# Three small moves of order in a fused attention and MLP kernel: one W2 sum, one z transpose, and the tail loads

## The chip, the cores and the metric

The kernel runs on one core of a Trainium2 chip. The metric is the device time of one execution in microseconds (us), the median over the runs of a kernel. A core has TensorE (PE in the profile; its weight loads are listed apart as PEld), VectorE (DVE), ScalarE (ACT), GpSimd (POOL) and SyncE (SP). Each works through its own instructions in the order in which they were issued; semaphores hold an instruction back until what it needs is done. Here SP issues nearly all of the DMA transfers.

## The reference

Eight batches of 576 positions, eight heads of 64. The first half is causal attention in a window of 64 keys; the second is a layer norm, two matrix products with a ReLU between them, and a residual sum.

```python
# q, k, v: [8, 8, 576, 64] float32
scores = q @ k.T / sqrt(64);  keep 0 <= (query - key) < 64, else -1e9
x = softmax(scores) @ v                    # -> [8, 576, 512], heads side by side
xn = (x - mean(x)) / sqrt(var(x) + 1e-6) * g_ln
out = x + relu(xn @ w_ch1) @ w_ch2         # w_ch1 [512, 2048], w_ch2 [2048, 512]
```

## The kernel before

**Groups.** The rows are worked on in nine groups. Groups 0 to 7 are the first 512 rows of each batch, as four row blocks (`kb`) of 128. Group 8, the "last group", gathers the remaining 64 rows of all eight batches, again as four row blocks, each of two batches; these are the "tails" 0 to 3.

**What one group needs.** For a batch: `load_qk` and `load_v` bring the float32 inputs, `cast_qk` and `cast_v` turn them into float16 on POOL, and `t_main` transposes q and k, on TensorE with an eviction by ACT or DVE, or for q from batch 3 on with a DMA that transposes on its way through the crossbar (L265). `s_pe` makes the scores (L349), `s_exp` the exponentials on ACT, `s_mask` the window on DVE, `b_pe` the product with v (L396); `part_vB` makes a shifted copy of v by DMA (L201, L203). `b_mult` and `b_stats` on DVE divide by the sums and take mean and variance; `z_step` on POOL writes the normalised rows z (L448 to L454). `zt_step` transposes z into `zT[g]`, the operand of the MLP: for groups 0 and 1, and for block 3 of groups 2, 3 and 5, with four TensorE transposes into one PSUM tile and a copy out of it (L478, L481 on ACT or L483 on DVE), for all other blocks with a crossbar DMA (L474).

**The MLP of a group.** It is a list of units (`mlp_units`): first the products with W1 (`l1`, L501; or in halves, `l1_half`, L642), then the products with W2. From group 1 on the W2 product is done with seven block products in place of eight (`stage` n, p, L575), which needs sums of blocks of the hidden rows (`s_sums`, L549) and of W2 (`w2_sums`, L836, into the tiles wT2, wT3 and wT4; the third of them, number 4, is made of W2 and of sum 2). The tiles wT2 to wT4 are also the landing place of three raw parts of W2, so that a sum can only be written after POOL has cast that part. The sums of the first half of the columns are made in group 0, those of the second half in group 1.

**The order.** A loop over the groups writes the order out by hand: `at(i, f, ...)` puts a piece of work for the next batch behind unit i of the present group. In group 2 the units 0 to 15 are the halves of W1, and 16 to 29 are the fourteen stages. So `at(22, ...)` of group 2 stands behind stage (6, 0), and the block transposes and tails that follow are for group 3, which is batch 3. Group 2 also carries the loads, casts and transposes of batch 4, and, as the last group's tail 0 is worked on in group 3, the work `load_tail`, `cast_tail` and `t_tail` for tail 0.

**PSUM for transposes.** `t_tile` gives out the tiles t0 and t1 in turn. From unit 20 on (17 in group 0) `tbank["shared"]` is set and it always gives t0, since t1 is then an accumulator of the W2 stages.

**DMA order on SP.** All the transfers named above stand in one queue on SP. Their completion is told by eight semaphores in turn, so each transfer is issued only after the one eight places ahead of it has landed. In group 2 the queue reads, in order: the loads of batch 4, the crossbar transfer of z block 0 of group 3, the six loads of tail 0 (L104 to L106), two crossbar transfers of q of batch 4 (L265), those of z blocks 1 and 2 (L474), the copies of v (L201, L203), four stores (L536), and the loads of batch 5.

Of the kernel before, what the change touches and what calls it, by code (L numbers as in the profile page):

```python
# [18 lines left out]
def kernel(  # L19
# [10 lines left out]
    nc = tc.nc  # L30
    B, H, S, D = q.shape
    DM = H * D
    HID = 4 * DM
    SM = 512
# [6 lines left out]
    XZ = 2  # L41
# [30 lines left out]
    def t_tile(shape, name):  # L72
        i = 0 if tbank["shared"] else tbank["n"] % 2
        tbank["n"] = i + 1
        return ps_t.tile(shape, FP16, tag=f"t{i}", name=name)
# [21 lines left out]
    def load_tail(i):  # L97
        tq = p_in.tile([128, H, D], FP32, tag="tq32", name=f"tq32_{i}", bufs=1)
        tk = p_in.tile([128, 2, H, D], FP32, tag="tk32", name=f"tk32_{i}", bufs=1)
        tv = p_in.tile([128, 2, H, D], FP32, tag="tv32", name=f"tv32_{i}", bufs=1)  # L100
        tail32[i] = (tq, tk, tv)
        for r in range(2):
            b = 2 * i + r
            nc.sync.dma_start(out=tq[64 * r:64 * r + 64], in_=q[b, :, SM:S, :].rearrange("h s d -> s h d"))  # L104
            nc.sync.dma_start(out=tk[:, r], in_=k[b, :, S - 128:S, :].rearrange("h s d -> s h d"))
            nc.sync.dma_start(out=tv[:, r], in_=v[b, :, S - 128:S, :].rearrange("h s d -> s h d"))  # L106

    def cast_tail(i):
        tq, tk, tv = tail32.pop(i)
# [358 lines left out]
    def zt_step(g, kb, eng="act"):  # L468
        z = zsd.pop((g, kb))
        if g not in zT:  # L470
            sfx = "r" if g == NGRP - 1 else ""
            zT[g] = p_grp.tile([128, NKC, 512], FP16, tag="zT" + sfx, name=f"zT_{g}", bufs=1 if sfx else 2)
        if XZ <= g and not (kb == 3 and g in (2, 3, 5)):
            nc.sync.dma_start_transpose(out=zT[g][:, :, 128 * kb:128 * kb + 128], in_=z)  # L474
            return
        ztp = t_tile([128, NKC, 128], f"ztp_{g}_{kb}")
        for kc in range(NKC):
            nc.tensor.transpose(out=ztp[:, kc, :], in_=z[:, 128 * kc:128 * (kc + 1)], identity=ident16)  # L478
        dst = zT[g][:, :, 128 * kb:128 * kb + 128]
        if eng == "act":  # L480
            nc.scalar.copy(out=dst, in_=ztp)  # L481
        else:
            nc.vector.tensor_copy(out=dst, in_=ztp)  # L483
# [362 lines left out]
    for i in range(8):  # L846
# [8 lines left out]
        out=mask[0:64], in_=mask[0:64], compare_op=ALU.is_gt, fill=0.0,  # L855
# [3 lines left out]
        out=mask[64:128], in_=mask[64:128], compare_op=ALU.is_ge, fill=0.0,  # L859
# [48 lines left out]
    b_step(0, 1)  # L908
    t_main(0, 1, 1, 0)
    zt_step(0, 0, "dve")  # L910
    keep_clock(2)
    s_mm(0, 2, True)
    zt_step(0, 1, "dve")
    keep_clock(1)
    b_step(0, 2)
# [31 lines left out]
    for g in range(NGRP):  # L947
# [7 lines left out]
        def at(i, f, *a):  # L955
            slots[min(i, len(slots) - 1)].append((f, a))
# [9 lines left out]
        b = g + 1  # L966
        if g == 0:
            at(0, w1_cast, 3, (1,), True)
            at(0, queue_up)
            at(1, zt_step, 0, 2, "dve")  # L970
            at(2, zt_step, 0, 3, "dve")
            at(11, t_main, 1, 0, 0, 1)
            at(12, t_main, 1, 1, 0, 1)
            at(16, s_pe, 1, 0)
            at(16, s_pe, 1, 1, False, "xps")
            at(16, s_exp, 1, 0, 0, 1)
            at(16, s_mask, 1, 0)
            at(17, s_exp, 1, 1, 0, 1)
            at(17, s_mask, 1, 1)
            for c in range(2):  # L980
                at(20, vB_cur, 1, c, 0)
                at(20, vB_prev, 1, c, 0)
            for i in (3, 2, 4):
                at(20, w2_sums, i, 0, 4)
            at(22, b_pe, 1, 0)
            at(22, b_rows, 1, 0)
            at(22, z_step, 1, 0)
            at(22, cast_act, 1, 0, 1)
            at(22, z_act, 1, 0)
            at(22, cast_qk, 1, 1, (1,))  # L990
            at(22, load_qk, 2, 1)
            at(22, load_v, 2, 0, 4)
            at(23, b_pe, 1, 1, "sc")
            at(23, b_rows, 1, 1)
            at(23, z_step, 1, 1)
            at(23, cast_v, 1, 2, 3)
            at(23, shift_v, 64, 2)
            at(23, shift_v, 0, 2)
            at(23, cast_v, 1, 3, 4)
            at(23, shift_v, 64, 3)  # L1000
            at(25, t_main, 1, 0, 1, 0)
            at(25, z_dve, 1, 1)
            at(26, lambda: tbank.update(n=0))
            at(26, t_main, 1, 1, 1, 0)
            at(27, zt_step, 1, 0, "dve")
            at(27, s_pe, 1, 2)
            at(27, s_pe, 1, 3, False, "xps")
            at(27, s_exp, 1, 2, 0, 1)
            at(27, s_exp, 1, 3, 0, 1)
            at(28, zt_step, 1, 1, "dve")  # L1010
            at(29, s_mask, 1, 2)
            at(29, s_mask, 1, 3)
        if g == 1:
# [38 lines left out]
            for j in range(4):  # L1052
                i = (13, 16, 22, 22)[j]
# [5 lines left out]
                i = (13, 17, 25, 27)[j]  # L1059
# [26 lines left out]
        if g == 2:  # L1086
            at(0, load_qk, 4, 1)
            at(0, s_exp, 3, 1, 1)
            at(1, z_act, 2, 3)
            at(1, s_mask, 3, 1)  # L1090
            at(2, b_pe, 3, 0)
            at(2, s_pe, 3, 2)
            at(2, s_pe, 3, 3, False, "t")
            at(5, zt_step, 2, 3, "act")
            for i, x in zip((2, 3, 4, 6), ((3, 0), (3, 1), (2, 0), (2, 1))):
                at(i, s_exp, 3, *x)
            at(3, load_v, 4, 0, 4)
            at(4, s_mask, 3, 3)
            at(4, b_rows, 3, 0)
            at(4, z_step, 3, 0)  # L1100
            at(7, s_mask, 3, 2)
            at(7, alloc_qkT, 4)
            at(7, after_mask, 3, 2)
            at(7, cast_qk, 4, 0)
            at(7, cast_qk, 4, 1)
            for j in range(1, 4):
                at(9, b_pe, 3, j, ("xps", "t", "sc")[j - 1])
                at((9, 10, 11)[j - 1], b_rows, 3, j)
                at((9, 10, 11)[j - 1], z_step, 3, j)
            for j, i in enumerate((8, 14, 18, 25)):  # L1110
                at(i, zt_step, 3, j)
        elif g > 1 and b < B:
            tail = TAILS.get(g)
            at(2, b_pe, b, 0)
            at(2, b_rows, b, 0)
            at(2, z_step, b, 0)
            at(2, s_pe, b, 2)
            at(2, s_exp, b, 2, 0, 1)
            at(3, s_mask, b, 2)
            if tail:  # L1120
                r, i = NGRP - 1, tail[0]
                at(2, s_pe, r, i, False, "t")
                at(4, s_exp, r, i, 0)
                at(5, s_exp, r, i, 1)
                at(5, s_mask, r, i)
                at(7, b_pe, b, 1)
                at(7, b_pe, r, i, "t")
                at(7, s_mm, b, 3)
                at(7, b_rows, b, 1)
                at(7, z_step, b, 1)  # L1130
                at(8, s_mask, b, 3)
                at(8, b_rows, r, i)
                at(9, z_step, r, i)
                at(12, b_pe, b, 2)
                at(12, b_pe, b, 3, "sc")
                at(16, zt_step, r, i)
            else:
                at(2, s_pe, b, 3, False, "t")
                at(4, s_exp, b, 3, 0)
                at(5, s_exp, b, 3, 1)  # L1140
                at(5, s_mask, b, 3)
                at(7, b_pe, b, 1)
                at(7, b_pe, b, 2, "t")
                at(7, b_pe, b, 3, "sc")
                at(7, b_rows, b, 1)
                at(7, z_step, b, 1)
            if g + 2 < B:
                at(5, alloc_qkT, g + 2)
                at(5, after_mask, *((NGRP - 1, tail[0]) if tail else (b, 3)))
                at(5, cast_qk, g + 2, 0)  # L1150
                at(5, cast_qk, g + 2, 1, (0,))
                at(11, cast_qk, g + 2, 1, (1,))
            for j, i in ((2, 12), (3, 19)):
                at(i, b_rows, b, j)
                at(i, z_step, b, j)
            for j in range(4):
                at((2, 14, 18, {3: 25, 5: 25}.get(b, 23))[j], zt_step, b, j)
# [7 lines left out]
        n = g + 2  # L1165
# [23 lines left out]
                at((15, 15, 20, 22)[i - 1], s_sums, 6, 8, i)  # L1189
        for n, i in enumerate(TAILS.get(g + 1, ())):  # L1190
            if n == 0:
                at(9 if g == 2 else 4, load_tail, i)
                at(24 if i < 2 else 18, cast_tail, i)
                at(27 if i < 2 else 22, t_tail, i, 0)
                at(29 if i < 2 else 22, t_tail, i, 1)
            else:
                at(25, load_tail, i)
# [48 lines left out]
```

## Time and profile before

| | us |
|---|---|
| median of 3 runs (lowest to highest) | 300.29 (299.87 to 301.8) |
| the profiled execution, its own time | 300.63 |
| its span, first to last instruction | 298.9 |
| PE busy in the span | 290.4 (97%) |
| DVE, POOL, ACT busy | 217.3, 163.1, 154.0 |
| mean granted TensorE clock | 0.998 |

The profile shows one execution. Busy time of an engine is the time in which at least one of its instructions ran; PE's matmuls are pipelined, so the time of a row of matmuls is read from the start of the first to the start of what follows. A timeline line gives the start, the length, the engine, the line of the code, the operation and its tiles, how many instructions are merged, and in brackets the engine's idle time before it with what ended that. For SP a line is the issue of a transfer, not its landing.

### The profile page before, as it was taken

The numbers are of one execution on the slowest core, as the hardware profiler recorded it, in microseconds if no ns is written. First come the engines' busy times: TensorE is split into PE (matmuls) and PEld (weight loads), VectorE is DVE, ScalarE is ACT, GpSimd is POOL, SyncE is SP. The second block draws the span as 40 slices with busy tenths as digits, with TensorE's granted clock in tenths as the row PEclk, the third lists the DMA queues.
The fourth block names the chain that finished last, engine by engine and source line by source line (L and its number), as shares of the span: only waits on it lengthen the run. The fifth ranks groups of instructions, "written<-read, shape, count | busy, mean of one in ns | idle before, by whom it ended". The sixth has DMA issues, their size and how long they took to land.

```text
span 298.9 us, 7820 instructions
## 1 busy us (share of the span) xinstructions
PE 290.4 (97%) x3183; PEld 206.4 (69%) x3183; DVE 217.3 (73%) x414; ACT 154.0 (52%) x260; POOL 163.1 (55%) x243
## 2 busy tenths in 40 slices
PE   7889999999999999999999999999999999999993
PEld 3557545888888888457854786469646854788883
DVE  2771388799993894489767865699568785779982
ACT  4576647677449525773276428841674056306500
POOL 4688877753850987189508860897048407024300
PEclk9999999999999999999999999999999999999999
DMA  7999999969979999999299998991729497003014
GB/s 190 260 380 339 385 283 280 261 213 301 181 170 290 246 174 161 271 272 180 45 285 279 190 174 278 285 162 39 220 52 179 71 177 195 20 18 143 1 37 106
DMA packets 113767, 58.24 MB, mean 195 GB/s; under 512 B 83137, under 2 KB 104705, under 8 KB 113730
## 3 DMA queue, kind: packets, MB, share of 16 engines
q1 hardware_dynamic: 113296, 57.34, 81.0%
q8 instruction: 25, 0.41, 0.6%
q10 hardware_dynamic: 434, 0.40, 0.4%
q14 instruction: 12, 0.10, 0.1%
HBM read 38.80 MB, written 9.44 MB: 161 GB/s over the span
## 4 chain that ended last, share of the span: by engine, by line
PE 66%; DMA 14%; DVE 8%; POOL 5%; SPq 3%; issue 2%; ACT 0%; POOLq 0%; DVEq 0%
PE hps L501 24%; PE pA L575 11%; PE pB L575 7%; PE pC L575 7%; DMA qk<-in_k_dram 6%; DMA w2s<-in_moe_w_ch_dram 3%; PE xps L396 3%; PE lA L698 2%; PE hph L642 2%; PE sc L349 2%; DMA out_dram<-xn 2%; POOL qk L154 2%; PE tp L276 2%; DMA tk<-in_k_dram 2%; DMA zT<-z 1%
## 5 line engine op out<-in xcount | busy, mean ns | idle before, releaser
L501 PE MATMUL hps<-zT,w1g 128*128 128x512 f16 x352 | 80.2, 379 | 0.4 <-DMA zT<-z 0.4
L505 ACT ACTIVATE hrT<-hps 128x512 f16<-128x512 f32 x88 | 52.8, 600 | 37.3 <-PE hps L501 34.3
L501 PEld LDWEIGHTS <-w1g 128*128 128x128 f16 x352 | 33.1, 98 | 38.6 <-issue 1.7
L575 PEld LDWEIGHTS <-sS 128*128 128x128 f16 x512 | 49.3, 98 | 5.7
L359 ACT ACTIVATE pt<-sc 128x512 f16<-128x512 f32 x72 | 39.8, 602 | 22.6 <-PE sc L349 22.1
L448 POOL TENSOR_SCALAR rsz<-mvg 128x1 f32<-128x1 f32 x32 | 10.5, 328 | 66.0 <-DVE mvg L429 63.4
L575 PEld LDWEIGHTS <-hrT 128*128 128x128 f16 x384 | 36.7, 98 | 7.0 <-ACT hrT L505 0.8
L369 DVE TENSOR_TENSOR pt<-pt,mask 128x1024 f16<-128x1024 f16 x32 | 24.4, 769 | 19.6 <-ACT pt L359 19.6
L642 PE MATMUL hph<-zT,w1g 128*128 128x256 f16 x320 | 38.0, 273 | 0.0
L154 POOL CAST qk<-qk 128x1024 f16<-128x1024 f32 x29 | 32.6, 1145 | 9.1 <-PE sc L349 6.0
L642 PEld LDWEIGHTS <-w1g 128*128 128x128 f16 x320 | 30.4, 98 | 4.7 <-POOL w1g L230 0.3
L575 PE MATMUL pC<-w2s,sS 128*128 128x256 f16 x256 | 31.1, 273 | 0.0
L575 PE MATMUL pA<-wT,sS 128*128 128x256 f16 x256 | 30.9, 273 | 0.0
L647 ACT ACTIVATE hrT<-hph 128x512 f16<-128x512 f32 x40 | 24.1, 606 | 11.0 <-PE hph L642 10.7
L257 ACT COPY qkT<-tp 128x1024 f16<-128x1024 f16 (+1 forms) x18 | 17.3, 963 | 23.2 <-PE tp L276 22.3
L549 DVE TENSOR_TENSOR sS<-hrT 128x1024 f16<-128x1024 f16 (+2 forms) x41 | 26.2, 638 | 2.1 <-ACT hrT L505 2.0
L420 DVE TENSOR_TENSOR xn<-xps,rcp 128x256 f32<-128x256 f32 (+1 forms) x50 | 25.8, 539 | 1.6 <-DMA out_dram<-xn 0.9
L426 DVE BATCH_NORM_STATS2 stats<-xn 128x6 f32<-128x512 f32 x36 | 25.0, 694 | 1.2
L454 POOL TENSOR_SCALAR z<-xn,rsz 128x512 f16<-128x512 f32 x24 | 22.4, 932 | 2.5
L449 POOL TENSOR_TENSOR rsz<-rsz,mhalf 128x1 f32<-128x1 f32 x32 | 20.6, 642 | 2.7
L182 POOL CAST vA<-v 128x1024 f16<-128x1024 f32 (+1 forms) x18 | 16.7, 945 | 4.2 <-DMA v<-in_v_dram 4.0
L416 DVE RECIPROCAL rcp<-xps 128x4 f32<-128x4 f32 (+1 forms) x50 | 7.9, 179 | 14.4 <-PE xps L396 14.4
(120 smaller groups left out, 421.9 us busy)
## 6 DMA issues: line engine op xcount, KB each, us to landing
qk<-in_q_dram SPq DMA_DIRECT2D x16, 512.0 KB, 6.0
qk<-in_k_dram SPq DMA_DIRECT2D x16, 512.0 KB, 6.9
out_dram<-xn SPq DMA_DIRECT2D x32, 256.0 KB, 3.6
v<-in_v_dram SPq DMA_DIRECT2D x28, 256.0 KB, 7.4
w2s<-in_moe_w_ch_dram SPq DMA_DIRECT2D x9, 512.0 KB, 8.5
w1s<-in_moe_w_ch_dram SPq DMA_DIRECT2D x4, 512.0 KB, 7.3
tk<-in_k_dram SPq DMA_DIRECT2D x8, 256.0 KB, 4.8
tv<-in_v_dram SPq DMA_DIRECT2D x8, 256.0 KB, 5.2
```

The lines of the kernel that those rows point to most:

```text
L154: nc.gpsimd.tensor_copy(out=dst[:, :].rearrange("p (a j) e d -> p a e j d", j=j), in_=t[:, :].rearrange("p (a e j d) -> p a e j d", e=2, j ...
L359: nc.scalar.activation(out=o, in_=i, func=AF.Exp, bias=0.0, scale=scale)
L369: nc.vector.tensor_tensor(out=ptv, in0=ptv, in1=mb, op=ALU.mult)
L420: nc.vector.tensor_tensor(out=xn[:, n * i:n * i + n], in0=xps[:, :, 0:D], in1=rcp_b, op=ALU.mult)
L426: nc.vector.bn_stats(out=stats, in_=xv)
L454: nc.gpsimd.tensor_scalar(out=z, in0=xv, scalar1=rs, scalar2=nm, op0=ALU.mult, op1=ALU.add)
L501: nc.tensor.matmul(out=hps, lhsT=w1g[:, kc, 128 * hc:128 * (hc + 1)], rhs=zT[g][:, kc, :], start=(kc == 0), stop=(kc == NKC - 1),)
L505: nc.scalar.activation(out=hrT[:, hc, :], in_=hps, func=AF.Relu, bias=0.0, scale=1.0)
L549: nc.vector.tensor_tensor(out=o, in0=x, in1=y, op=op)
L575: nc.tensor.matmul(out=o, lhsT=a[:, c, 128 * p:128 * p + 128], rhs=wv[:, c, :], start=(first and (p == 0 or split_c) and c == 0), stop=(c ...
L642: nc.tensor.matmul(out=hps[:, e], lhsT=w1g[:, kc, 128 * hc:128 * (hc + 1)], rhs=zT[g][:, kc, 256 * half:256 * half + 256], start=(kc == 0) ...
L647: nc.scalar.activation(out=hrT[:, 2 * i:2 * i + 2, 256 * half:256 * half + 256], in_=hps, func=AF.Relu, bias=0.0, scale=1.0)
```

## The change

Three edits. The third W2 sum of group 0 (`w2_sums` 4, columns of the first half) is no longer issued at unit 20, behind sums 3 and 2, but at unit 27, between the DVE copies of the transposed blocks 0 and 1 of group 1. Row block 2 of group 3 is transposed on TensorE, at unit 22 of group 2 and with ACT's copy, in place of the crossbar transfer at unit 18. And `load_tail(0)` moves from unit 9 to unit 15 of group 2, behind the crossbar transfers of q of batch 4 and of z block 1; the six loads of every tail now come in the order q, q, k, k, v, v in place of q, k, v, q, k, v.

```diff
@@ load_tail
-        for r in range(2):
+        for n in range(6):
+            r = n % 2
             b = 2 * i + r
-            nc.sync.dma_start(out=tq[64 * r:64 * r + 64], in_=q[b, :, SM:S, :].rearrange("h s d -> s h d"))
-            nc.sync.dma_start(out=tk[:, r], in_=k[b, :, S - 128:S, :].rearrange("h s d -> s h d"))
-            nc.sync.dma_start(out=tv[:, r], in_=v[b, :, S - 128:S, :].rearrange("h s d -> s h d"))
+            if n < 2:
+                nc.sync.dma_start(out=tq[64 * r:64 * r + 64], in_=q[b, :, SM:S, :].rearrange("h s d -> s h d"))
+            else:
+                t, x = (tk, k) if n < 4 else (tv, v)
+                nc.sync.dma_start(out=t[:, r], in_=x[b, :, S - 128:S, :].rearrange("h s d -> s h d"))
@@ zt_step
-        if XZ <= g and not (kb == 3 and g in (2, 3, 5)):
+        if XZ <= g and not ((kb == 3 and g in (2, 3, 5)) or (g, kb) == (3, 2)):
             nc.sync.dma_start_transpose(out=zT[g][:, :, 128 * kb:128 * kb + 128], in_=z)
             return
@@ group 0
-            for i in (3, 2, 4):
+            for i in (3, 2):
                 at(20, w2_sums, i, 0, 4)
...
             at(27, zt_step, 1, 0, "dve")
+            at(27, w2_sums, 4, 0, 4)
             at(27, s_pe, 1, 2)
@@ group 2
-            for j, i in enumerate((8, 14, 18, 25)):
+            for j, i in enumerate((8, 14, 22, 25)):
                 at(i, zt_step, 3, j)
@@ tails
             if n == 0:
-                at(9 if g == 2 else 4, load_tail, i)
+                at(15 if g == 2 else 4, load_tail, i)
```

In the built program TensorE has eight rows more (four weight loads and four transposes), ahead of the last eight transposes of k of batch 4, the first of which now also waits for ACT; ACT has one copy more, SP one transfer less, and DVE and POOL the same instructions as before.

## Prediction

> **What bounds the kernel now.** I read the busy totals first, then TensorE's list of waits, then the timelines of PE and its neighbours at the two places that the change touches (43 to 54 us, 102 to 121 us). The page and the list of waits of the whole span (total us, times, longest us):
>
> ```profile
> PE 290.4 (97%) x3183; PEld 206.4 (69%) x3183; DVE 217.3 (73%) x414; ACT 154.0 (52%) x260; POOL 163.1 (55%) x243
> ...
> PE hps L501 <- DMA zT<-z: 0.4, 1, 0.4
> PE ch L659 <- POOL w2s L243: 0.3, 1, 0.3
> ```
>
> TensorE is the bound. Of the 8.5 us in which it isn't busy, most lies at the two ends of the span. Between 45 and 294 us these two lines are nearly all: one wait for W2's last part, one for the first product of group 3. Each matmul added in there lengthens the run by its own time, each wait ended shortens it, and no wait that can be ended is near 3 us. About 1% (3 us) is what a measurement of this kernel can tell from no change.
>
> The place of edit 1, in the timelines of DVE and POOL:
>
> ```profile
> 43.48 0.69 DVE L836 TENSOR_TENSOR wT<-w2s,wT 128x1024 f16<-128x1024 f16 x1
> ...
> 51.28 0.41 DVE L483 COPY zT<-ztp 128x512 f16<-128x512 f16 x1
> 53.09 0.42 DVE L483 COPY zT<-ztp 128x512 f16<-128x512 f16 x1 [1.41 <-PE ztp L478]
> ...
> 37.91 1.04 POOL L243 CAST w2s<-wT 128x1024 f16<-128x1024 f32 x1 [0.27 <-DMA wT<-in_moe_w_ch_dram]
> 43.57 1.51 POOL L243 CAST w2s<-w2s 128x1024 f16<-128x1024 f32 x1 [0.71 <-DMA w2s<-in_moe_w_ch_dram]
> 51.14 1.34 POOL L197 CAST vB<-v 64x512 f16<-64x512 f32 x2
> ```
>
> The reader is to see that the third sum and the last W2 cast run together at 43.5, that this cast takes 1.51 us where another takes 1.04, and that DVE stands idle for 1.41 us at 51.7.
>
> The place of edits 2 and 3, in the timelines of PE, ACT and SP:
>
> ```profile
> 111.27 0.61 PE L276 MATMUL tp<-ident,qk 128*128 128x128 f16 x8
> 114.34 0.39 PE L478 MATMUL ztp<-ident,z 128*128 128x128 f16 x4
> 114.56 1.91 PE L575 MATMUL pA<-wT,sS 128*128 128x256 f16 x16
> 116.40 0.78 PE L349 MATMUL sc<-qkT,qkT 64*128 64x64 f16 x32
> 119.09 0.61 PE L307 MATMUL tpk<-ident,tk 128*128 128x128 f16 x8
> ...
> 114.76 0.58 ACT L481 COPY zT<-ztp 128x512 f16<-128x512 f16 x1 [1.83 <-PE ztp L478]
> ...
> 108.64 0.62 SPq L105 DMA_DIRECT2D tk<-in_k_dram  x1
> 110.60 4.01 SPq L265 DMA_TRANSPOSE qkT<-qk  x2
> 114.70 2.56 SPq L474 DMA_TRANSPOSE zT<-z  x2
> ```
>
> SP issues q's two crossbar transfers only at 110.6, behind the tail loads, and z's two at 114.7. By the DMA view the second of q lands at 113.4+3.2 = 116.6, just as the scores that read it run (116.40): those 32 matmuls take 0.78 us where the same row at 148.51 takes 0.64, a stall of **0.14**. The second of z lands at 116.0+4.0 = 120.0, and PE waits **0.40** for it.
>
> **Edit 1.** Nothing is added. With the sum gone from 43.48, I take the cast at its undisturbed 1.04: it ends at 44.61 and not 45.08. PE finishes what stands before the waiting matmul at 44.87, so its wait of 0.26 goes: **-0.26**, and no more, since PE has no other wait there. At the new place the sum starts at 51.73 and takes 0.69 alone, ending at 52.42, ahead of the next DVE copy (53.09, or 52.83 with PE 0.26 earlier): hidden by DVE's pause. Queued behind it is that copy, for which group 1's first products wait. The other bound is the first sum, which ran beside a POOL cast and took 1.52: it would end at 53.25, the copy at 53.67, and the products that could start at 53.50 would start 0.17 late. So -0.26 to -0.09; I take -0.26, as the two POOL casts at the new place are short (0.67 each). The sum's own readers come only with the W2 stages of group 1, at 72.48.
>
> The Trainium skill, SBUF — State Buffer, section "SBUF: two separate sides", says that DVE and GpSimd share a port pair which the first to start holds for its whole instruction, the other standing still. The trace agrees: 44.17 (the sum's end) plus 1.04 is 45.21, close to the cast's 45.08. By that rule the moved sum could stand behind the second short cast until 52.48, end at 53.17 and give back 0.09.
>
> **Edit 2.** It removes a transfer: SP's issue (1.2 us of the 2.56) and the wait of 0.40. It adds four transposes, a copy on ACT, and a wait. The four cost what the same four cost at 114.34: 0.22 to the next matmul. But at unit 22 tile t0 is the only transpose tile, and the eight transposes of k, queued right behind, need it: they wait for ACT's copy. From the row at 114.34, the copy starts 0.42 after the first transpose and takes 0.58; 0.05 more passes from POOL's cast end at 45.08 to PE's start at 45.13, which I take for the release. So the eight start **1.05** after the four began, where before they began at once: **+1.05**, of which 0.83 is PE standing still, as PE runs in order. ACT is free (idle 2.93 us before its copy at 111.92). z is ready: POOL writes block 2 at 109.39 to 110.15, more than 0.8 us ahead. The bounds are +0.22, were the eight not held, and +1.10 with a copy of 0.63 (the longest such, at 95.33); I take 1.05, since the built program gives the first of the eight a wait on ACT. All behind it on PE moves with it; the next user of t0 comes 3.07 us later and isn't held. Gone is **-0.40**, if the other transfers into zT[3] are in time, below.
>
> The Trainium skill, TensorE: Matmul & The Clock Gate, "Part 4: PE-mode transpose", gives some 275 ns to one 128x128 transpose in a kernel and says that its result must be copied out of PSUM. By that, an estimate from the page, the four would cost 1.10 in place of 0.22 and the whole 301.4. The row (0.22 for four) decides for the size, and the copy out is just what makes the stall above.
>
> **Edit 3.** Moved are six loads, past two transfers of q and one of z. The two of q now follow at 104.10 (POOL's casts for them end at 103.8). Batch 5's pair, with no tail ahead, took 3.04 to issue and 4.1 to 5.0 to land: landing by 112, 4 us ahead of the scores. So **-0.14**. z block 1 (POOL done at 106.9) is issued at 107.1 to 108.4, landing by 113 at the 4.2 that block 0 took. Then the tails: six issues took 6.4 us before, 104.1 to 110.5, so now 108.4 to 114.8; the second k load, fourth in order, is issued between 110.5 and 113.1, lands 5.0 later, by 118.1, and is cast in 1.04. PE asks for k at 119.09+1.05-0.40 = 119.74, edit 1's and edit 3's gains taken off, so a landing by 118.65 is hidden. v comes last and is needed near 128; POOL has nothing after these casts until 125.4. The v copies, queued behind, wait for POOL's casts (until 114.9) and land some 3 us later, ahead of the product at 122.8. The order within the other tails costs nothing: tail 1's last k load landed at 173.7, POOL cast it at 176.7. Lower bound -0.14; upper bound in the rivals.
>
> **Sum:** -0.26 + 1.05 - 0.40 - 0.14 = **+0.25**. The profiled execution took 300.63 (span 298.9 and 1.73 around it, which I leave as it is), so 300.88 for that one; it lies 0.34 above the median of 300.29, so the median becomes **300.5**. With the bounds of edits 1 and 2 alone, 299.7 to 300.8.
>
> **Rivals.** *The stall does not bite* (faster): were the eight transposes not held, the four cost 0.22 and the sum is -0.58, 299.7. For it: PE issues a row of transposes in 0.45 us, before the profile shows their ends, so starts and ends are partly modelled. Against it: the single tile and the wait in the program.
>
> *The tail loads come too late* (slower): they now stand behind crossbar transfers, in a queue whose issues already took up to 4 us each for batch 4's v. If the second k load is issued at 113.1 and takes 8.9 us as the slowest v load did, it lands at 122.0, the cast ends at 123.0, and PE waits 3.3 us ahead of t_tail's k transposes: 303.8. It decides from a landing after 118.65. Against it: the loads themselves took 3.6 to 6.4, and q and k now come before v.
>
> *The change does not do what it says*: block 1's transfer lands late in its turn and takes over the 0.40. Then 300.9. Against it are the 7 us between its landing and PE's need.
>
> **How the numbers follow.** The forecast 0.66, the stall absent 0.14, the late tails 0.12, the wait kept 0.08. Only the late tails pass 1%, and about half of their landings do; beside that I leave something for what the view of waits doesn't show in either direction. Faster by over 1%: 0.04, since PE's waits don't hold 3 us; within 1%: 0.85; slower: 0.11. The range is from 299.4 (the stall absent, and 0.3 for medians that differ) to 302.2 (half way to the late tails).
>
> **What would show it.** Right: PE's wait at L659 gone and the cast near 1.04; a PE idle of about 0.8 us ahead of L276 near 111, put down to ACT's L481; the idle at 120 gone; the scores near 116 back to 0.64. Wrong: no idle at L276 (then faster), or PE idle ahead of L298 or L307 put down to POOL's casts of tq or tk (then slower); a sum at 51.7 of 1.5 us and PE waiting at L642 would undo edit 1.

## The result, and the profile after

| | before | changed |
|---|---|---|
| median, us | 300.31 (22 runs, 299.57 to 301.8) | 301.40 (22 runs, 301.11 to 302.53) |
| the profiled execution, its own time, us | 300.63 | 301.29 |
| its span, us | 298.9 | 299.6 |

The ratio is 1.0037, with a 95% interval of 1.0026 to 1.0048: slower by 1.1 us, within 1%, the forecast having been 0.25. The time lies in the range that was given, though the size was forecast too small. Lines are numbered three higher than before from `cast_tail` on.

The busy line of the page and TensorE's whole list of waits (total us, times, longest us), of the changed kernel:

```profile
PE 291.2 (97%) x3187; PEld 206.9 (69%) x3187; DVE 219.1 (73%) x414; ACT 154.4 (52%) x261; POOL 164.6 (55%) x243
...
PE warm L872 <- DVE mhalf L856: 1.1, 1, 1.1
PE ztp L481 <- DVE z L443: 0.8, 1, 0.8
PE tp L279 <- ACT zT L484: 0.7, 1, 0.7
PE xps L399 <- ACT pt L362: 0.5, 2, 0.3
```

Both waits that the change was to end are gone (L501 for z, L659 for W2). In their place stands TensorE's wait for ACT's copy of block 2, as forecast. The 0.8 at L481 is not of the change: it falls at 16 us, in group 0, where both programs are the same, and a second profile of before has it too, at 0.4.

TensorE and ACT around unit 22 (timelines of the changed kernel):

```profile
111.39 0.39 PE L481 MATMUL ztp<-ident,z 128*128 128x128 f16 x4
112.45 0.61 PE L279 MATMUL tp<-ident,qk 128*128 128x128 f16 x8 [0.67 <-ACT zT L484]
117.58 0.64 PE L352 MATMUL sc<-qkT,qkT 64*128 64x64 f16 x32
120.14 0.61 PE L310 MATMUL tpk<-ident,tk 128*128 128x128 f16 x8
120.58 2.79 PE L504 MATMUL hps<-zT,w1g 128*128 128x512 f16 x12
...
111.82 0.59 ACT L484 COPY zT<-ztp 128x512 f16<-128x512 f16 x1 [2.71 <-PE ztp L481]
```

From the start of the four transposes to that of the eight it is 112.45-111.39 = 1.06 (1.05 forecast). The scores take 0.64 in place of 0.78. The first product of group 3 stood before at

```profile
120.10 1.25 PE L501 MATMUL hps<-zT,w1g 128*128 128x512 f16 x5 [0.40 <-DMA zT<-z]
```

From the tail's k transposes to this product it is 0.44, where it was 120.10-119.09 = 1.01: 0.57 gained. That is more than the 0.40 of the list, because an idle time counts only from the modelled end of the matmul ahead, and a start can follow a start sooner than that.

DVE and POOL at the moved sum, changed kernel:

```profile
51.67 0.76 DVE L839 TENSOR_TENSOR wT<-w2s,wT 128x1024 f16<-128x1024 f16 x1
52.85 0.42 DVE L486 COPY zT<-ztp 128x512 f16<-128x512 f16 x1 [0.42 <-PE ztp L481]
54.38 2.13 DVE L372 TENSOR_TENSOR pt<-pt,mask 128x1024 f16<-128x1024 f16 x2
...
51.94 0.97 POOL L200 CAST vB<-v 64x512 f16<-64x512 f32 x1
54.33 1.04 POOL L157 CAST qk<-qk 128x1024 f16<-128x1024 f32 x1
```

The masks and the q cast of before:

```profile
54.63 1.45 DVE L369 TENSOR_TENSOR pt<-pt,mask 128x1024 f16<-128x1024 f16 x2
...
53.90 1.04 POOL L154 CAST qk<-qk 128x1024 f16<-128x1024 f32 x1
```

The sum is hidden on DVE as forecast (0.76, the copy in time). But POOL's cast beside it takes 0.97, where two such casts took 1.34 together before, so that POOL's queue behind it is late: the q cast of batch 2 stands at 54.33 where it stood at 53.90. There it meets DVE's two masks, which take 2.13 where they took 1.45. The second product with v waits for the second mask. The starts before and behind the two products (TensorE, before and then changed):

```profile
56.17 0.22 PE L396 MATMUL xps<-vB,pt 128*64 128x65 f16 x1
...
56.82 1.92 PE L642 MATMUL hph<-zT,w1g 128*128 128x256 f16 x16
```

```profile
55.98 0.22 PE L399 MATMUL xps<-vB,pt 128*64 128x65 f16 x1
...
56.23 0.19 PE L399 MATMUL xps<-vB,pt 128*64 128x65 f16 x1
...
56.56 0.22 PE L399 MATMUL xps<-vB,pt 128*64 128x65 f16 x1
...
56.95 1.49 PE L645 MATMUL hph<-zT,w1g 128*128 128x256 f16 x12
```

The pair takes 0.97 in place of 0.65, with a hole from 56.23 to 56.56. The list of waits doesn't show it: the modelled end of the last matmul ahead (56.23+0.19) covers more than half of the hole, and the 0.14 that is left makes no entry. What edit 1 gained at 45 us is given back here. In what follows this chain, from the sum over POOL's casts and DVE's masks to TensorE, is called the relay.

Below, a gain or loss "on TensorE" is always read in this way: the start of the same matmul in the one profile less that in the other.

### The profile page after: what moved, and what is told of

It is laid out like the page before. It is cut to its first block, busy times and chain, and to the rows that moved or that the text cites. A ratio compares the mean times of both kernels' runs of the same rounds, so it can differ in the third digit from the quotient of the medians.

```text
span 299.6 us, 7822 instructions
## 1 busy us (share of the span) xinstructions
PE 291.2 (97%) x3187; PEld 206.9 (69%) x3187; DVE 219.1 (73%) x414; ACT 154.4 (52%) x261; POOL 164.6 (55%) x243
## 4 chain that ended last, share of the span: by engine, by line
PE 95%; DVE 2%; ACT 1%; issue 0%
PE hps L504 26%; PE pA L578 14%; PE hph L645 11%; PE pB L578 10%; PE pC L578 9%; PE xps L399 4%; PE sc L352 4%; PE ch L662 4%; PE tp L279 3%; PE lA L701 2%; PE warm L872 2%; PE lC L701 1%; PE ch L516 1%; PE ztp L481 1%; DVE pt L372 1%; ACT pt L362 1%
## 5 line engine op out<-in xcount | busy, mean ns | idle before, releaser
L372 DVE TENSOR_TENSOR pt<-pt,mask 128x1024 f16<-128x1024 f16 x32 | 25.0, 789 | 19.2 <-ACT pt L362 19.2
L552 DVE TENSOR_TENSOR sS<-hrT 128x1024 f16<-128x1024 f16 (+2 forms) x41 | 26.9, 656 | 1.8 <-ACT hrT L508 1.8
L399 PEld LDWEIGHTS <-pt 128*64 128x64 f16 x576 | 11.5, 110 | 9.4 <-issue 5.1
```

The costliest lines, as they stand in the source:

```text
L372: nc.vector.tensor_tensor(out=ptv, in0=ptv, in1=mb, op=ALU.mult)
L399: nc.tensor.matmul(out=tiles[h // n][64 * r:64 * r + 64, h % n, :D + 1], lhsT=pt[:, par, hp, r, :], rhs=rhs, start=True, stop=True)
L552: nc.vector.tensor_tensor(out=o, in0=x, in1=y, op=op)
```

## The experiments

The theory was that of the terms: a stall of 1.05 added, three waits ended, which add up. The rivals that came out of the profile after: edit 1 is given back by the relay over POOL; and the ended waits are in some executions of before only, so that most have little to gain. Medians are against runs of before on the same chip.

**Each edit alone.** The diffs are the three parts of the change.

*Edit 1 alone* (`for i in (3, 2)` at unit 20, `at(27, w2_sums, 4, 0, 4)`).

> Only edit 1: the third W2 sum moved, all else as before. Differences from before, in us. The forecast (the wait for the last W2 cast goes, the sum is hidden in DVE's pause): -0.26, TensorE ahead by that from 45 us to the end. Rival, given back by a relay: the moved sum holds up POOL's casts for vB at 51.7 by some 0.4, these push POOL's cast of q to 54.3, that one holds up DVE's two masks, and TensorE waits some 0.3 for the second product with v near 56.3: -0.26 + 0.37 = about +0.1, TensorE level with before again from 57 us on.

Measured 300.57 against 300.25, ratio 1.0007 (0.9993 to 1.0022). On TensorE -0.32 at the last products with W2 near 45 us, and +0.36 up to the second product with v, so level from 57 us on: the relay, alone and in full. And this profile, in which nothing of z was touched, has no wait for z at 120 and none in the scores at 116. TensorE's list of waits from 40 us to the end is one line, a wait for q at 178 us, in group 4:

```profile
PE sc L349 <- DMA qkT<-qk: 0.3, 1, 0.3
```

*Edit 2 alone* (block 2 in `zt_step`'s condition, at unit 22).

> Only edit 2: row block 2 of group 3 transposed on TensorE at unit 22, tails and sum as before. The forecast: +1.05 for the transposes and the wait for ACT's copy, less the wait of 0.40 for z at 120 and the 0.14 in the scores (both lie later on TensorE than the stall of 0.83 and are covered by it): +0.5. Rival, that most executions of before have no such waits and the profiled one had them by chance: +1.05.

Measured 300.84 against 300.25, ratio 1.0011 (0.9999 to 1.0023). On TensorE +1.07 from the four transposes to the eight, +0.20 ahead of the four, and -0.70 at the scores and at 120: +0.57. The 0.20 is a wait for z itself, which the forecast had 0.8 us early: in this execution POOL wrote block 2 in 1.09 us in place of 0.76 and ended at 111.64, the four starting at 111.69. Median and profile lie near the forecast's +0.5, but the interval reaches below 1, so this run doesn't decide against +1.05 either.

*Edit 3 alone* (`load_tail(0)` at unit 15, the loads' new order).

> Only edit 3: the six loads of tail 0 behind the crossbar transfers of q and of z block 1, z block 2 by crossbar behind the tails. The forecast: the 0.14 in the scores goes; z block 2 is issued near 115 and lands at 117.5 to 119, just in time, so the 0.40 goes too: -0.54, or -0.14 if block 2 keeps its lateness. Rival, that most executions of before have no such waits: 0.0. If the tails come too late: TensorE idle ahead of the transposes of k of the tail, above 0.

Measured 300.40 against 300.25, ratio 1.0014 (0.9997 to 1.0030). In the profile the scores and z are in time (-0.67 together), and TensorE waits for no tail. The median shows no gain: a sign of the second theory. Five of the twelve runs took 301.15 us or more, against one of the 35 of before; what these waited for isn't recorded.

**The stall.** The changed kernel with block 2 two units later, when t0 is free:

```diff
-            for j, i in enumerate((8, 14, 22, 25)):
+            for j, i in enumerate((8, 14, 24, 25)):
```

> The changed kernel with row block 2 transposed at unit 24 in place of 22, two units behind the transposes of k, so that tile t0 is free when it is asked for. The theory of the stall: the four transposes cost 0.22 and not 1.05, so 0.83 less than the changed kernel; against before -0.58 by the forecast, -0.2 if edit 1 gives its gain back, +0.3 if the waits of before are mostly not there. Rival, that the stall costs nothing because something else sets the end: as the changed kernel, +1.1.

Measured 300.20 against 300.25, ratio 1.0004 (0.9992 to 1.0017); the changed kernel run again (below) was 301.39. On TensorE the four transposes cost 0.24 in place of 1.06, and the gains at 116 and 120 (-0.70) are there in the same way. The stall is shown: two units earlier or later are worth about 1 us, and all else is alike.

**Before and changed again.**

> The kernel before, as it is, beside itself. Ratio 1 within the interval; it tells what five rounds can tell apart. Its second profile tells whether the waits on which the forecast's gains rest (0.26 at the last W2 cast, 0.14 in the scores near 116, 0.40 for z at 120) belong to most executions or came by chance in the first profile. The forecast takes them to be there: all three within 0.1. Rival: one or more of them missing, and the profiled execution faster than the 300.63 of the first by as much.

> The kernel before once more, for its third profile and for the spread of its executions: TensorE's wait for z at 120 between 0 and 0.8, the wait for the last W2 cast between 0 and 0.4; time of the profiled execution follows them.

> The changed kernel, as it is, on the chip of the other runs of this call: +1.1 against before by the first measurement. If the single edits add up (sum moved +0.3, transposes +0.6, tails +0.15 by medians), +1.05. By the profiles' terms (stall +1.07, scores and z -0.70, W2 -0.35, relay +0.36) +0.4.

Before again: 300.19 against 300.46, ratio 0.9996 (0.9983 to 1.0009); a third time 300.50 against 300.30, ratio 0.9999 (0.9987 to 1.0011). Five rounds thus tell apart some 0.13%, 0.4 us, and not only the 1% that the prediction took. The changed kernel again: 301.39 against 300.46, ratio 1.0043 (1.0026 to 1.0060); the medians of the single edits (0.32, 0.59 and 0.15) add up to 1.06. The two profiles of before took 300.97 and 301.07 us. Their lists of waits between 40 and 125 us, whole, the second run's first:

```profile
PE hps L501 <- DMA zT<-z: 0.6, 1, 0.6
PE ch L659 <- POOL w2s L243: 0.2, 1, 0.2
```

```profile
PE hps L501 <- DMA zT<-z: 0.7, 1, 0.7
PE ch L659 <- POOL w2s L243: 0.4, 1, 0.4
```

All three profiled executions of before have the wait for z, and all three took longer than their kernel's median. Of the seven profiles in which z block 2 goes by crossbar, the three of before and one more (below) have it, with 0.4 to 0.8; edits 1 and 3 alone and the next experiment have none. Of the eight in which the third sum stands where it was, five have the wait for W2's last cast (0.2 to 0.4) and three have none. What decides about W2's wait can be seen in all eight. Where the third sum starts first (43.39 to 43.71), the cast beside it ends 0.90 us after the sum, in all five, and TensorE waits. Where the cast starts first, by 0.11 to 0.27 us, in the other three, it takes 1.04 to 1.08 and the sum is the one that is slow, as in the last experiment below:

```profile
43.50 1.45 DVE L836 TENSOR_TENSOR wT<-w2s,wT 128x1024 f16<-128x1024 f16 x1
...
43.37 1.04 POOL L243 CAST w2s<-w2s 128x1024 f16<-128x1024 f32 x1 [0.49 <-DMA w2s<-in_moe_w_ch_dram]
```

The eight programs are the same up to there, so this wait comes and goes with the landing of W2's last part. The waits for z and in the scores (0.14, 0.26 and 0.04 in the three profiles of before) go with the place of SP's queue: in the three of before, z's transfer was issued at 116.0 to 116.2 and landed 4.0 to 4.3 later; with edit 1 alone and in the next experiment it was issued at 115.3 and landed 3.9 to 4.2 later, just in time. Why SP was 0.7 us earlier in those two isn't shown. Both have the third sum moved, and the version with sum and tails moved has the wait again: that z's wait, too, comes by chance is likely, but not shown for the kernel of before itself, which had it three times of three.

**The relay.** Edit 1 alone, but the sum behind the two masks:

```diff
+            at(29, s_mask, 1, 3)
+            at(29, w2_sums, 4, 0, 4)
```

> Only edit 1, but with the sum two units later, behind DVE's two masks near 56 in place of ahead of the copy near 52.8. The theory of the relay: POOL's casts for vB are no longer held up, the q cast and the masks come in time, the wait in the second product with v (0.36) is not there, and the gain of some 0.3 at 45 stays: -0.3 against before, 0.3 less than with the sum alone moved to unit 27. DVE is then later by up to 0.7 at the next division, which TensorE has room for until the transposes of z near 61 to 63; if it has not, a wait there takes some 0.1 to 0.3 back. Rival, that TensorE's wait near 56.3 is not from the sum: the wait stays, level with before.

Measured 300.42 against 300.46, ratio 0.9998 (0.9985 to 1.0012). DVE and POOL of this kernel:

```profile
54.34 1.78 DVE L369 TENSOR_TENSOR pt<-pt,mask 128x1024 f16<-128x1024 f16 x2
56.04 0.68 DVE L836 TENSOR_TENSOR wT<-w2s,wT 128x1024 f16<-128x1024 f16 x1
...
53.93 1.04 POOL L154 CAST qk<-qk 128x1024 f16<-128x1024 f32 x1
```

POOL's q cast is back at 53.93, the masks end at 56.12 and not at 56.51, and TensorE is still 0.27 ahead at the second product with v: the hole was the moved sum's. It then loses 0.24 at 63.15, at the transposes of z block 3, since DVE is now late there. Neither of the two places tried is free on DVE in this stretch; each makes another reader wait.

**Both without stall.** Edit 3 with block 2 by crossbar, and the sum behind the masks.

> Edit 3 with all row blocks of group 3 but the last by crossbar as before, and the sum behind the masks: the version without the stall and without the relay. By the profiles' terms -0.70 (scores and z) and -0.3 (sum) = -1.0 against before. If the gains of edit 3 are there only in some executions, as its median of +0.15 suggests: between -0.3 and 0.

Measured 301.08 against 300.46, ratio 1.0010 (0.9996 to 1.0024): a miss. The profile shows the wait for z at its largest:

```profile
120.58 1.69 PE L504 MATMUL hps<-zT,w1g 128*128 128x512 f16 x7 [0.77 <-DMA zT<-z]
```

Block 2's transfer, queued behind the tails in this version, was issued at 114.76 and is as late as before. Edit 3 without edit 2 doesn't end this wait reliably. Nor did the sum behind the masks keep its gain: of the 0.32 at 45 us, 0.22 were lost at 49.5, where the k cast on POOL had waited for its load, and 0.12 at the second product with v, with POOL's q cast at 54.33 again though no sum held it up. So the moved sum is one cause of a late q cast, and not the only one.

**The parts together.** The changed kernel without edit 1; the same with block 2 at unit 24; and block 2 at unit 24 as the only change:

> The changed kernel without edit 1: the third W2 sum stays where it was, transposes at unit 22 and tails as changed. If the moved sum costs more than it brings in most executions (relay +0.36 always, the wait for the last W2 cast only in some), 0.1 to 0.36 less than the changed kernel, 301.1 to 301.3 and +0.7 to +1.0 against before; TensorE has no wait in the second product with v near 56.5. If edit 1 is level (-0.3 and +0.36), as the changed kernel; if it gains, more.

> Row block 2 at unit 24 and the tails as changed, the sum where it was: no stall, no relay, no wait for z at 120. The four transposes cost 0.22 in every execution. If z's wait (0.4 to 0.8) comes in a part of the executions of before alone, the median is level with before (-0.2 to +0.2) and the executions lie closer together, with none of the upper group of before at 300.7 to 301.1 that comes from z; against the same with the sum moved (300.2, -0.05) 0.0 to 0.3 less.

> Only row block 2 on TensorE at unit 24; sum and tails as before. It removes one crossbar transfer and costs 0.22. z block 1 then is the last by crossbar, behind the tails, landing near 117 and in time: the wait at 120 goes in this one too. Against before -0.2 (0.22 less 0.40 in the executions that have it), the scores near 116 still wait 0.14 for q. If instead the tails' place is what makes z late: the wait at 120 stays, for block 1, and the kernel is +0.2.

| | median (before on that chip) | ratio |
|---|---|---|
| changed, without edit 1 | 301.07 (300.30) | 1.0028 (1.0019 to 1.0038) |
| the same, block 2 at unit 24 | 300.07 (300.30) | 0.9998 (0.9988 to 1.0007) |
| block 2 at unit 24 alone | 299.79 (300.30) | 0.9984 (0.9971 to 0.9996) |

By the medians edit 1 costs some 0.3 (1.1 less 0.77; 0.32 alone; 0.18 between the two versions at unit 24), always the same way, but each time within the intervals, so this isn't shown. The place of the transposes is worth 1.0, beyond the intervals. The second version's runs lie closer together, as expected, but for one of its eleven at 301.02. The last version is the only one below before beyond its interval, by 0.5 us by the medians and by little at the interval's end, one of twelve such intervals in these experiments; it has the tails in their old place. The wait in the scores that was expected there is not in its profile (0.64). In this profile SP issues block 1 at 113.27, behind the tails, and it lands in time: here one crossbar transfer less was enough, with the tails where they had been. None of the seven profiles with block 2 on TensorE has a wait for z. TensorE's stretch in this version:

```profile
113.19 0.39 PE L478 MATMUL ztp<-ident,z 128*128 128x128 f16 x4
113.41 1.04 PE L575 MATMUL pC<-w2s,sS 128*128 128x256 f16 x8
114.28 0.39 PE L478 MATMUL ztp<-ident,z 128*128 128x128 f16 x4
...
119.35 1.89 PE L501 MATMUL hps<-zT,w1g 128*128 128x512 f16 x8
```

The matmuls follow the four transposes after 0.22, and the copy of t0 is done while eight products run.

## Why the prediction was right in kind and too small

- **TensorE is the bound, and what is put in there lengthens the run**: right. Each step on TensorE near 111 and 120 us is still there at its last product, 0.5 us later than before.
- **Edit 2, the stall, +1.05**: right, 1.06 in the profile and 1.0 between the medians of units 22 and 24. Of the page's 275 ns for a transpose (the Trainium skill, TensorE: Matmul & The Clock Gate, "Part 4: PE-mode transpose") the trace shows nothing: four took 0.22 to the next matmul. That the result must be copied out of PSUM is what cost.
- **Edit 3**: the landings were right (the second k load issued at 110.9, cast at 115.59 without a wait of POOL; v late, POOL waiting 1.7 for it, and nobody for POOL). The scores' 0.14 went, with q landing at 109.5, 8 us ahead of them. But it is missing as well in four profiles with the tails in their old place (edits 1 and 2 alone, the sum behind the masks, unit 24 alone), so that edit 3 ended it isn't shown. The rival of the late tails didn't come true in the changed kernel's profiles.
- **Edit 1**: the gain at 45 us was right (0.33 for the 0.26 forecast), and the sum is hidden on DVE. The step that failed is its bound of -0.09: "queued behind it is that copy" looked at DVE's queue alone. The engine that stood still beside the sum was POOL, and what is queued there reached TensorE by way of two masks: +0.32 here, and the pair takes 0.97 in all four profiles with the sum at unit 27. The Trainium skill, SBUF — State Buffer, "SBUF: two separate sides" (the one that starts second stands still until the other's instruction ends) was drawn on with DVE as the loser. The traces agree with the rule: in all fourteen profiles the second mask ends 1.14 us after POOL's q cast (here 56.51 after 55.37), however late that cast is. But the price lay with the other loser.
- **The sum for the profiled execution**: -0.33 + 0.32 + 1.06 - 0.14 - 0.57 = +0.34, where +0.25 was forecast; two errors (0.3 given back, 0.2 more gained) nearly cancel. TensorE's first product of group 3 came 0.48 later; the rest, some 0.1, was there at 44 us, ahead of all that was changed. Its last product is 0.5 later, the execution 0.66, of which 0.16 came behind the last product.
- **From that execution to the median**: this step failed most, "it lies 0.34 above the median of 300.29, so the median becomes 300.5". The forecast took the waits of one execution, which was slower than 15 of the 22 runs, as those of all, and subtracted them from the median; none of its rivals has executions without them. W2's wait is missing in three of the eight profiles with the sum in its old place and z's in three of the seven with block 2 by crossbar, while the stall is in all four profiles with the transposes at unit 22 and the relay in all four with the sum at unit 27. An execution of before with none of the three waits has nothing to gain from the change and pays 1.06 + 0.32 = 1.4. The median's 1.1 lies between that and the 0.34 of the profiled pair, and the lowest runs of the two kernels, 299.57 and 301.11, are 1.5 apart. In numbers: 0.66 between the two profiled executions, 0.32 by which that of before was above its median, and 0.11 by which that of the changed kernel was below its own make up the 1.09. How often each wait comes in unprofiled runs wasn't measured: that missing waits make the difference is argued from the times.
- **The range**: 301.40 lies in it by luck. Its upper end of 302.2 was set by the late tails, which did not come; by the bounds of edits 1 and 2 alone the time was to be at most 300.8, and it passed them by 0.6.

## What to carry to other kernels

A transpose put ahead of other transposes costs its neighbours the copy out of PSUM when they share one tile: 1.06 us here, against 0.22 with eight products between. A piece moved into an engine's pause must be checked against the engine that it stops beside it, and what stands queued there; the idle time of its own engine tells only half. A wait seen in one profile is worth only the share of executions that have it: W2's was decided by which of two instructions started first, by 0.1 to 0.3 us. A cost on the bounding engine was in every profile.

## What the runs showed of the hardware

The same program's wait for a crossbar transfer of 128x512 float16 values at 120 us was 0.4, 0.6 and 0.7 us in three executions, and none in two others that differ only in the place of the W2 sum, some 60 us earlier; the transfer took 3.9 to 4.3 us to land in all five, and its issue came 0.7 us earlier in the two. A DVE sum of two float16 operands of 128x1024 and a POOL cast of 128x1024 slowed each other according to which started first: the cast took 1.28 to 1.51 us and the sum 0.69 when the sum started first, the cast 1.04 to 1.08 and the sum 1.35 to 1.47 when the cast did. A short hole in TensorE's issue (0.33 us at 56 us) is invisible in the list of waits, as the modelled ends of the small matmuls ahead (0.19 each, issued every 0.02) reach over more than half of it; only the starts of the matmuls tell.
